# One bank and one reduce for the last query tile's row maxima, their minimum taken on the transposed row, and the rows' transfers issued by SyncE from head 22 on

## The chip, the cores and the metric

The kernel runs on one core of a Trainium2 chip. A core has TensorE (PE: matmuls and, beside them, weight loads, PEld), VectorE (DVE), ScalarE (ACT), GpSimd (POOL) and SyncE (SP). Each has a queue of its own, which it works through in order; DMA transfers are issued from the queues of ACT, POOL and SP and carried out by 16 DMA engines. The metric is the time on the device in microseconds (us), the median of several executions.

## The reference: what is computed

Attention in 8 batches of 8 heads, 576 positions, head size 64, with a mask by blocks of 64 (a query block sees its own and earlier key blocks), then a feed-forward part over the 4608 tokens, 512 wide inside 2048:

```python
scores = scale * np.matmul(q, k.transpose(0, 1, 3, 2))
mask = block_i >= block_j                 # blocks of 64 positions
scores = np.where(mask, scores, -1000000000.0)
scores = scores - np.max(scores, axis=-1, keepdims=True)
attn = np.exp(scores); attn = attn / (np.sum(attn, axis=-1, keepdims=True) + 1e-09)
x = (attn @ v) as 4608 x 512
h = x @ w_in                              # 512 x 2048
sp = np.maximum(h, 0.0) + np.log1p(np.exp(-np.abs(h)))
out = (h * erf(sp)) @ w_out               # 2048 x 512
```

What matters here is the maximum of each query's visible scores, which is subtracted before the exponential.

## The kernel before

The 64 heads (8 x 8) are passed in a loop over n; queries are cut into five tiles of 128 (the last has 64). `load_qk` brings a head's queries and keys (L383 and L385 from POOL's queue, L384 the copy `st` from SP's queue) into one of four buffers `qks[n % 4]`, and POOL works out their low parts (L388, L389). One partition of such a buffer, D + 4, is reserved for the negated maxima of the queries: a head's scores are computed twice, first in `maxes` to find the maxima, and then in `probs` with the maxima as one more row of the contraction (K = D + 5), so that PE itself subtracts them.

`maxes(n)` has the scores of the five query tiles in PSUM banks (L400), tile 0 and 1 in one bank, tiles 2 and 3 in one each, and the last tile's 64 queries in two banks: its 576 keys don't fit a bank of 512, so they are two halves of 288. DVE reduces each to a negated maximum per query (L403) in a column of `mx`: columns 0 to 3 for the first tiles, 5 and 6 for the halves of the last, of which L428 takes the minimum into column 4. Then PE transposes the five columns (L430), ACT rounds them into `mt`, five rows of 128 (L432), and ACT issues one transfer that lays these rows one behind the other into the head's buffer (L433, called the row). `probs(n)` can't begin before that has landed: its first product of each key tile, L446, reads the row; a second product L447 adds the low parts, and ACT takes the exponential (L451). L495 multiplies them with the values.

In iteration n of the head loop the steps of several heads are merged by fractional positions: the load of head n + 3, the maxima of head n + 2, the row of head n + 1, the probabilities of head n, and the products of earlier heads with the values. Beside them run, from head 9 on, the MLP's tiles of 256 tokens (up L190, the polynomial for erf(softplus) on ACT L159 to L162, DVE L163 to L165, ACT L166 and POOL L167, down L199, the sum with parts stored in `part_d` L240 to L249), and until head 23 the splitting of the weights into 16-bit parts (L112 to L147, by integer operations of DVE and activations of ACT). A scheduler turns priorities into the final order of each engine's queue, so an edit can move instructions that it doesn't touch. Ahead of the loop stand the maxima of heads 0 and 1, and head 0's row. The loads of raw weights and values wait for a one-element copy from tile 3's column of `mx` (L112 and L325), which keeps them behind the heads' loads. In iterations 0 and 1 there are dummy matmuls, ten each (L647), called "warm" in the trace.

Of the kernel before, what the change touches and what calls it, by code (L numbers as in the profile page):

```python
# [9 lines left out]
F32 = mybir.dt.float32  # L10
# [4 lines left out]
ALU = mybir.AluOpType  # L15
AX = mybir.AxisListType
# [7 lines left out]
def f32(ap):  # L24
    return ap.bitcast(F32)
# [7 lines left out]
def tile_attention_moe(ctx: ExitStack, tc: tile.TileContext, qk, v, w, maskrows, sels, out):  # L33
    nc = tc.nc
    B, H, D4, S = qk.shape
    D = D4 // 4
    NT, DM = out.shape
    NF = w.shape[0]
    P = 128
    NCC = DM // P  # L40
    SCALE = 0.125
    NQ = H // 4
# [221 lines left out]
    NB = 4  # L264
    qks = [wpool.tile([P, 4 * S + 64], F32R, name=f"qk{i}", bufs=1) for i in range(NB)]
# [28 lines left out]
    with tc.tile_pool(name="apool", bufs=2) as apool, tc.tile_pool(name="spool", bufs=1) as spool, \  # L294
            tc.tile_pool(name="ps_a", bufs=4, space=PSUM) as ps_a:
        pstage = [spool.tile([P, n], F32, name=f"p32_{i}") for i, n in enumerate(PN)]
        rss = [spool.tile([P, SH], F32, name=f"rs{i}") for i in range(3)]
        mxs = [spool.tile([P, 7], F32, name=f"mx{i}") for i in range(2)]

        def memsets():  # L300
            nc.gpsimd.memset(pstage[0][64:128, 768:], 0.0)
# [7 lines left out]
        def bank(name):  # L309

            turn.append(0)
            k = len(turn) % 8 if not loaded else 0
            if k in (2, 5):
                return ps_h.tile([P, 512], F32, tag="h", name=name)
            if k in (3,):
                return ps_o.tile([P, 512], F32, tag="o", name=name)
            return ps_a.tile([P, 512], F32, tag="a", name=name)
# [75 lines left out]
        def maxes(n):  # L393

            mx, K = mxs[n % 2], D + 4
            kh, qh = part(n, 2), part(n, 3)

            def mm(dst, i, k0, w_):
                r = min(P, S - i * P)
                nc.tensor.matmul(dst[:r, :w_], lhsT=qh[:K, i * P : i * P + r], rhs=kh[:K, k0 : k0 + w_], start=True, stop=True)  # L400

            def red(col, src, r=P):
                nc.vector.tensor_reduce(out=mx[:r, col : col + 1], in_=src, axis=AX.X, op=ALU.max, negate=True)  # L403

            def a():
                s = bank(f"s01_{n}")
                mm(s, 0, 0, 256)
                mm(s[:, 256:], 1, 0, 256)
                red(0, s[:, :128])
                red(1, s[:, 256:])  # L410

            def b():
                s = bank(f"s2_{n}")
                mm(s, 2, 0, 384)
                red(2, s[:, :384])

            def c():
                s = bank(f"s3_{n}")
                mm(s, 3, 0, 512)
                red(3, s)  # L420

            def d(j):
                s = bank(f"s4_{n}_{j}")
                mm(s, 4, 288 * j, 288)
                red(5 + j, s[:64, :288], 64)

            def e():
                nc.vector.tensor_reduce(out=mx[:64, 4:5], in_=mx[:64, 5:7], axis=AX.X, op=ALU.min)  # L428
                pt = bank(f"mt{n}")
                nc.tensor.transpose(out=pt[:5, :P], in_=mx[:, :5], identity=ident)  # L430
                mt = apool.tile([5, P], F32R, tag="mt", name=f"mt_{n}")
                nc.scalar.copy(mt, pt[:5, :P])  # L432
                nc.scalar.dma_start(f32(qks[n % NB][D + 4 : D + 5, 3 * S :]).rearrange("o (i p) -> o i p", p=P), f32(mt))  # L433

            return [a, b, c, lambda: d(0), lambda: d(1), e]

        def probs(n, out):

# [165 lines left out]
        def next_raw(src=None):  # L604
            if len(raws) < len(HALVES):
                fs = HALVES[len(raws)]
                raws[fs] = load_raw(*fs, apool, src)

        for n in range(2):
            *steps, rows[n] = maxes(n)  # L610
            for f in steps:
                f()
            if n == 0:
                v32 = load_v(0, 0, mxs[0][:1, 3:4])
                rows.pop(0)()
            next_raw(mxs[n][:1, 3:4])
        def late(kind, steps):

            def run(f):
# [30 lines left out]
        for n in range(N + 3):  # L650
            lists = []
            if n + NB - 1 < N:
                load, low = load_qk(n + NB - 1)
                lists += [(late("load", [load]), 0, LQ), (late("low", [low]), LQ, 1)]
            if n + 2 < N:
                *steps, rows[n + 2] = maxes(n + 2)
                lists.append((late("max", steps), 0, 1))
            if n + 1 in rows:
                lists.append((late("max", [rows.pop(n + 1)]), 0, 0.6))
            if n < N:  # L660
                prs[n] = []
                lists.append((late("prob", probs(n, prs[n])), 0, 1))
            qd = n // 4 + 1
            if n < 2:
                lists.append(([lambda v0=v32: scale_v(0, 0, *v0), lambda v0=v32: vs.__setitem__(0, prep_v(0, 0, *v0))][n : n + 1], 0.6, 0.8))
            if n % 4 == 1 and qd < N // 4:
                v32 = load_v(*divmod(qd, NQ), mxs[(n + 1) % 2][:1, 3:4])
            if n % 4 == 2 and qd < N // 4:
                lists.append((late("v", [lambda qd=qd: scale_v(*divmod(qd, NQ), *v32)]), 0, 1))
            if n % 4 == 3 and qd < N // 4:  # L670
                lists.append((late("v", [lambda qd=qd: vs.__setitem__(qd, prep_v(*divmod(qd, NQ), *v32))]), 0, 1))
            if n % 2 == 0 and 2 <= n <= N:
                j = n // 2 - 1
                qd, pp = divmod(j, 2)
                usbs[j] = apool.tile([P, S], F32, tag="usb", name=f"usb{j}", bufs=2)
                steps = pv(qd, pp, [prs.pop(2 * j), prs.pop(2 * j + 1)], vs[qd], usbs[j], rss[j % 3])
                lists.append((late("pv", steps), 0, 1))
                if pp == 1:
                    normals[n + 1] = qd
            if n in normals:  # L680
                qd = normals.pop(n)
                b, q_ = divmod(qd, NQ)
                lists.append((late("norm", normalise(b, q_, [usbs.pop(2 * qd), usbs.pop(2 * qd + 1)], [rss[2 * qd % 3], rss[(2 * qd + 1) % 3]])), 0.2, 0.8))
                if q_ == NQ - 1:
                    lists.append((late("norm", [lambda b=b: scale_b(b)]), 0, 0.2))
                    ready_at[n + 1] = (b + 1) * S // T
            ready = ready_at.get(n, ready)
            for _ in range(TOF.get(n, 0)):
                lists.append((late("conv", [conv]), 0, 1))
            if n in SCALE_AT:  # L690
                lists.append(([lambda n=n: scale_group(SCALE_AT[n])], 0, 0.1))
            if n in SPLIT:
                lists.append((late("conv", [split_next] * SPLIT[n]), 0.1, 1))
            if n < 2:
                lists.append(([warm] * WARM, 0, 1))
            lists.append((late("moe", [lambda: moe1(ready)] * RATE[0 if n < 10 else 1 if n < 20 else 2]), 0, 1))
            merge(*lists)
# [42 lines left out]
```

## Time and profile before

| | us |
|---|---|
| median of 3 executions | 1251.46 (1250.63 to 1252.27) |
| the profiled execution | 1253.77 |
| its span | 1252.0 |
| TensorE busy | 1169.7 (93%) |
| weight loads (PEld) | 811.0 (65%) |
| ScalarE busy | 865.4 (69%) |
| VectorE busy | 791.9 (63%) |
| GpSimd busy | 515.9 (41%) |

The span is the time between the first and the last instruction in the profile, and the execution's own time lies 1.77 us above it. Rows of groups read: line, engine, operation, out<-in with partitions x elements, count, then busy time, mean ns of one, and idle time ahead of them with what ended it. Rows of a timeline read: start, duration, engine, line, and in square brackets the idle time before with its releaser. ACTq and SPq are the queues' DMA issues. PE's busy time counts a matmul from its start to its modelled end, and neighbours overlap.

### The profile page before, as it was taken

What the parts mean: (1) busy time and instruction counts of PE and PEld (TensorE: products, weight loads), DVE (VectorE), ACT (ScalarE), POOL (GpSimd) and SP (SyncE); (2) the same over time, 40 slices, a digit from 0 to 9 for tenths busy, and PEclk for the clock granted to TensorE, in tenths of its full rate; (3) what the DMA queues carried; (4) which work ended last, traced back from release to release, by engine and by line L of the source; (5) the groups of instructions that cost most, each with busy time, mean ns of one, the idle gap of its engine ahead of it and who ended that gap; (6) DMA issues with size and microseconds to landing.
All of it is one profiled execution on the core that took longest, in us unless ns stands there. A gap on an engine that the chain in (4) does not pass through costs nothing.

```text
span 1252.0 us, 23446 instructions
## 1 busy us (share of the span) xinstructions
PE 1169.7 (93%) x9018; PEld 811.0 (65%) x9018; DVE 791.9 (63%) x1457; ACT 865.4 (69%) x1699; POOL 515.9 (41%) x486
## 2 busy tenths in 40 slices
PE   5788699989999999999999899999999999999896
PEld 2465466666666767767767677766777766666563
DVE  4677689787577666676657667666666644343433
ACT  1465577687676777877777677777777876666664
POOL 6455446545343444445444353545443313121211
PEclk9876799999999999999999999999999999999999
DMA  9988569744544455364454455455554121121211
GB/s 218 250 208 190 124 181 234 195 101 117 112 128 110 115 125 128 100 147 120 99 124 116 118 119 130 112 124 128 112 137 108 45 78 53 60 76 35 64 55 51
DMA packets 95741, 151.73 MB, mean 121 GB/s; under 512 B 7738, under 2 KB 44922, under 8 KB 95630
## 3 DMA queue, kind: packets, MB, share of 16 engines
q1 hardware_dynamic: 69840, 93.34, 25.7%
q0 software_dynamic: 25120, 56.66, 22.6%
q8 instruction: 71, 1.16, 0.4%
q10 hardware_dynamic: 670, 0.23, 0.2%
q14 instruction: 40, 0.33, 0.1%
HBM read 121.66 MB, written 28.31 MB: 120 GB/s over the span
## 4 chain that ended last, share of the span: by engine, by line
PE 49%; DVE 20%; ACT 18%; DMA 7%; issue 4%; POOL 1%; DVEq 0%; SPq 0%; POOLq 0%; ACTq 0%
PE m_h L190 16%; PE o L199 15%; PE u L495 5%; DVE m_r L163 4%; DVE m_r L164 4%; DVE m_r L165 3%; ACT m_r L160 3%; ACT m_r L162 3%; ACT m_r L161 3%; ACT m_r L159 3%; PE t L446 3%; PE s L400 3%; PE t L447 2%; DMA qk<-qk 2%; DMA qk<-mt 2%
## 5 line engine op out<-in xcount | busy, mean ns | idle before, releaser
L190 PE MATMUL m_h<-xh,w 128*128 128x256 f16 x2304 | 476.1, 276 | 19.5 <-DVE m_r L165 12.2
L190 PEld LDWEIGHTS <-w 128*128 128x128 f16 x3456 | 328.3, 99 | 158.1 <-issue 31.2
L199 PE MATMUL o<-w,m_gh 128*128 128x512 f16 x1152 | 334.1, 382 | 12.2 <-DVE pt L240 4.9
L167 POOL TENSOR_TENSOR m_gl<-m_r,m_gh 128x512 f16<-128x512 f32 x144 | 171.8, 1193 | 391.1 <-ACT m_gh L166 340.6
L190 PE MATMUL m_h<-xl,w 128*128 128x256 f16 x1152 | 316.8, 275 | 0.5 <-DMA xl<-x_d 0.5
L403 DVE TENSOR_REDUCE mx<-s 64x1 f32<-64x288 f32 (+4 forms) x384 | 174.5, 469 | 131.3 <-PE s L400 130.5
L163 DVE SCALAR_TENSOR_TENSOR m_r<-m_r,m_r 128x512 f32<-128x512 f32 x144 | 112.8, 783 | 197.3 <-ACT m_r L162 190.8
L199 PE MATMUL o<-w,m_gl 128*128 128x512 f16 x576 | 203.7, 384 | 0.3 <-POOL m_gl L167 0.3
L451 ACT ACTIVATE p<-t 128x288 f32<-128x288 f32 (+4 forms) x384 | 144.6, 384 | 79.4 <-PE t L447 69.1
L166 ACT CAST m_gh<-m_r 128x512 f16<-128x512 f32 x144 | 88.9, 617 | 157.2 <-DVE m_r L165 154.4
L446 PE MATMUL t<-qk 69*128 69x288 f32 (+4 forms) x384 | 168.2, 439 | 13.0 <-DMA qk<-mt 6.8
L400 PE MATMUL s<-qk 68*64 68x288 f32 (+3 forms) x384 | 150.1, 423 | 22.8 <-DMA qk<-qk 19.8
L159 ACT ACTIVATE m_r<-m_h,c,bs 128x512 f32<-128x512 f32 (+3 forms) x192 | 124.1, 666 | 44.5 <-PE m_h L190 41.4
L388 POOL TENSOR_TENSOR qk<-st,qk 64x576 fp32r<-64x576 f32 x64 | 95.9, 1499 | 127.2 <-DMA qk<-qk 124.5
L199 PEld LDWEIGHTS <-m_gh 128*128 128x128 f16 x1152 | 100.2, 98 | 67.6 <-issue 12.3
L164 DVE SCALAR_TENSOR_TENSOR m_r<-m_r 128x512 f32<-128x512 f32 x144 | 122.6, 852 | 3.3
L447 PE MATMUL t<-qk 128*128 128x288 f32 (+4 forms) x384 | 120.0, 313 | 0.0
L463 DVE TENSOR_TENSOR p<-p,p 128x832 f16<-128x832 f32 x80 | 81.7, 1022 | 58.0 <-ACT p L462 57.9
L389 POOL TENSOR_TENSOR qk<-st,qk 64x576 fp32r<-64x576 f32 x64 | 98.4, 1538 | 39.2 <-DMA qk<-qk 29.1
L161 ACT ACTIVATE m_r<-m_r,c 128x512 f32<-128x512 f32 x144 | 103.8, 721 | 2.7 <-ACT m_r L160 0.7
L162 ACT ACTIVATE m_r<-m_r,c 128x512 f32<-128x512 f32 x144 | 103.7, 720 | 2.3 <-ACT m_r L161 0.3
L160 ACT ACTIVATE m_r<-m_r,c 128x512 f32<-128x512 f32 x144 | 103.7, 720 | 1.6
(99 smaller groups left out, 1454.8 us busy)
## 6 DMA issues: line engine op xcount, KB each, us to landing
qk<-qk POOLq DMA_DIRECT2D x64, 432.0 KB, 5.0
st<-qk SPq DMA_DIRECT2D x64, 288.0 KB
qk<-qk POOLq DMA_DIRECT2D x64, 288.0 KB, 5.6
raw<-w SPq DMA_DIRECT2D x32, 512.0 KB
v<-v SPq DMA_DIRECT2D x16, 640.0 KB
x_d<-xs POOLq DMA_DIRECT2D x32, 288.0 KB, 3.3
xh<-x_d SPq DMA_DIRECT2D x36, 256.0 KB
xl<-x_d SPq DMA_DIRECT2D x36, 256.0 KB
```

Of the source, the lines that this page charges most:

```text
L159: nc.scalar.activation(r0s[:, :, lo:hi], h[:, :, lo:hi], AF.Tanh, bias=const(p1), scale=bss[b][g][:, 0:1])
L161: nc.scalar.activation(r0, r1, AF.Square, bias=const(b2), scale=a2)
L163: nc.vector.scalar_tensor_tensor(out=r0, in0=r0, scalar=c4, in1=r1, op0=ALU.add, op1=ALU.mult)
L164: nc.vector.scalar_tensor_tensor(out=r0, in0=r0, scalar=c5, in1=r0, op0=ALU.add, op1=ALU.mult)
L167: nc.gpsimd.tensor_tensor(out=gl, in0=r0, in1=gh, op=ALU.subtract)
L190: nc.tensor.matmul(h[:, k, :], lhsT=wf[:, a, sl], rhs=x[:, cc, :], start=cc == 0 and i == 0, stop=cc == NCC - 1 and i == 2)
L199: nc.tensor.matmul(o[c], lhsT=a[:, sl], rhs=wf[:, b_, :], start=u == u0 and k == 0 and not lo and b_ == 2, stop=u == u1 - 1 and k == nu - ...
L400: nc.tensor.matmul(dst[:r, :w_], lhsT=qh[:K, i * P : i * P + r], rhs=kh[:K, k0 : k0 + w_], start=True, stop=True)
L403: nc.vector.tensor_reduce(out=mx[:r, col : col + 1], in_=src, axis=AX.X, op=ALU.max, negate=True)
L446: nc.tensor.matmul(s[:kk, :w_], lhsT=kh[:K, ks], rhs=qh[:K, q0 : q0 + w_], start=True, stop=False)
L447: nc.tensor.matmul(s[:kk, :w_], lhsT=klh[:, ks], rhs=qhl[:, q0 : q0 + w_], start=False, stop=True)
L451: nc.scalar.activation(p32s[part][:kk, c : c + w_ - skip], s[:kk, skip:w_], AF.Exp, scale=SCALE)
```

## The change

`mx` shrinks from seven columns to five: tile i is reduced into column (i + 1) % 5, so the last tile is in column 0. The last tile uses one bank: a product of 128 queries (the last 128) with keys 288 to 575 fills rows 0 to 127, then the product of the last 64 queries with keys 0 to 287 overwrites rows 0 to 63. So rows 64 to 127 hold the last queries' scores with the later keys, rows 0 to 63 those with the earlier ones, and one reduce of 128 partitions takes both. After the transpose, row 0 of `mt` holds the two partial maxima side by side, and DVE takes their minimum there (a piece of 64 elements on one partition). The row goes out as two transfers: four rows of 128, which don't need that minimum, and the 64 elements of row 0. Both are issued by ACT for heads below 22 and by SP from 22 on. The copies that hold the loads back read column 4, again tile 3's.

```diff
-        mxs = [spool.tile([P, 7], F32, name=f"mx{i}") for i in range(2)]
+        mxs = [spool.tile([P, 5], F32, name=f"mx{i}") for i in range(2)]
...
-            def red(col, src, r=P):
-                nc.vector.tensor_reduce(out=mx[:r, col : col + 1], in_=src, axis=AX.X, op=ALU.max, negate=True)
+            def red(i, src):
+                col = (i + 1) % 5
+                nc.vector.tensor_reduce(out=mx[:, col : col + 1], in_=src, axis=AX.X, op=ALU.max, negate=True)
...
-            def d(j):
-                s = bank(f"s4_{n}_{j}")
-                mm(s, 4, 288 * j, 288)
-                red(5 + j, s[:64, :288], 64)
+            def d():
+                s = bank(f"s4_{n}")
+                nc.tensor.matmul(s[:, :288], lhsT=qh[:K, S - P :], rhs=kh[:K, 288:], start=True, stop=True)
+                mm(s, 4, 0, 288)
+                red(4, s[:, :288])
 
             def e():
-                nc.vector.tensor_reduce(out=mx[:64, 4:5], in_=mx[:64, 5:7], axis=AX.X, op=ALU.min)
                 pt = bank(f"mt{n}")
                 nc.tensor.transpose(out=pt[:5, :P], in_=mx[:, :5], identity=ident)
                 mt = apool.tile([5, P], F32R, tag="mt", name=f"mt_{n}")
                 nc.scalar.copy(mt, pt[:5, :P])
-                nc.scalar.dma_start(f32(qks[n % NB][D + 4 : D + 5, 3 * S :]).rearrange("o (i p) -> o i p", p=P), f32(mt))
-
-            return [a, b, c, lambda: d(0), lambda: d(1), e]
+                nc.vector.tensor_tensor(out=mt[:1, :64], in0=f32(mt[:1, :64]), in1=f32(mt[:1, 64:]), op=ALU.min)
+                row = f32(qks[n % NB][D + 4 : D + 5, 3 * S : 3 * S + S])
+                dma = (nc.scalar if n < 22 else nc.sync).dma_start
+                dma(row[:, : 4 * P].rearrange("o (i p) -> o i p", p=P), f32(mt[1:]))
+                dma(row[:, 4 * P :], f32(mt[:1, :64]))
+
+            return [a, b, c, d, e]
...
-            next_raw(mxs[n][:1, 3:4])
+            next_raw(mxs[n][:1, 4:5])
```

The scheduler moves instructions in response. The first place is PE's queue at the very start. In the names, s01_1 are the scores of head 1's tiles 0 and 1, s4 those of the last tile, mt0 the transposed maxima of head 0, qk1 head 1's buffer. Before, from row 5 of the queue on:

```order
L400 MATMUL s4_0_1_216<-qk0_128 64x288
L400 MATMUL s4_1_1_245<-qk1_129 64x288
L400 MATMUL s4_1_0_242<-qk1_129 64x288
L647 LDWEIGHTS ones32_78
L647 MATMUL warm_251<-ones32_78 32x512
L647 LDWEIGHTS ones32_78
L647 MATMUL warm_251<-ones32_78 32x512
L400 MATMUL s01_2_263<-qk2_130 128x256
L430 MATMUL mt0_223<-ident_77,mx0_146 5x128
L400 MATMUL s01_1_231<-qk1_129 128x256 x2
L400 MATMUL s2_1_236<-qk1_129 128x384
```

After, the same stretch, where the line of "..." stands for nineteen more pairs of a weight load and a warm matmul:

```order
L425 MATMUL s4_0_213<-qk0_128 128x288
L400 MATMUL s4_0_213<-qk0_128 64x288
L400 MATMUL s01_1_230<-qk1_129 128x256 x2
L400 MATMUL s2_1_235<-qk1_129 128x384
L652 LDWEIGHTS ones32_78
L652 MATMUL warm_248<-ones32_78 32x512
...
L400 MATMUL s01_2_260<-qk2_130 128x256 x2
L400 MATMUL s3_1_238<-qk1_129 128x512
L431 MATMUL mt0_220<-ident_77,mx0_146 5x128
L425 MATMUL s4_1_241<-qk1_129 128x288
L400 MATMUL s4_1_241<-qk1_129 64x288
L451 MATMUL t0_0_0_256<-qk0_128 128x288
```

The transpose of head 0 stood behind two of the twenty warm matmuls and now stands behind all of them, and head 0's first product with the row (L451 of the changed kernel) follows three instructions later.

The second place is DVE's queue at the start. Before, head 0's minimum (L428) is taken ahead of all of head 1's reduces:

```order
L403 TENSOR_REDUCE mx0_146<-s4_0_1_216 64x1
L325 COPY v0_0_219<-mx0_146 1x1
L112 COPY raw0_0_228<-mx0_146 1x1
L428 TENSOR_REDUCE mx0_146<-mx0_146 64x1
L403 TENSOR_REDUCE mx1_147<-s4_1_0_242 64x1
L403 TENSOR_REDUCE mx1_147<-s4_1_1_245 64x1
```

After, head 0's minimum (L434) comes behind all five of head 1's reduces:

```order
L404 TENSOR_REDUCE mx0_146<-s4_0_213 128x1
L325 COPY v0_0_217<-mx0_146 1x1
L112 COPY raw0_0_227<-mx0_146 1x1
L404 TENSOR_REDUCE mx1_147<-s01_1_230 128x1 x2
L404 TENSOR_REDUCE mx1_147<-s2_1_235 128x1
L404 TENSOR_REDUCE mx1_147<-s3_1_238 128x1
L404 TENSOR_REDUCE mx1_147<-s4_1_241 128x1
L434 TENSOR_TENSOR mt_0_222<-mt_0_222 1x64
L112 COPY raw0_1_245<-mx1_147 1x1
```

The minimum moved from before the transpose to behind it, and on DVE it stands behind head 1's reduces of s3 and s4.

The third place is SP's queue where the rows' transfers come to it. The first two of them in the changed kernel, with what stands around them (v32 are values, xh and xl the attention's output read back, ob a part sum that is stored):

```order
L326 DMA v32_3_0_3042<-v 128x1280
L437 DMA qk2_130<-mt_22_3086 1x4x128
L438 DMA qk2_130<-mt_22_3086 1x16x4
L384 DMA st_26_3492<-qk 128x576
L243 DMA part_d_58<-ob0_2_0_3172 128x512
L243 DMA part_d_58<-ob0_2_1_3234 128x512
L222 DMA xl1_1_3351<-x_d_57 128x4x256
L222 DMA xh1_1_3349<-x_d_57 128x4x256
L384 DMA st_27_3657<-qk 128x576
L437 DMA qk3_131<-mt_23_3335 1x4x128
L438 DMA qk3_131<-mt_23_3335 1x16x4
```

Without those four rows the stretch is the same in the kernel before, where ACT issues them: the transfers of head 23 stand behind the load `st` of head 27.

More of the change, by code (lines that the diff above doesn't have):

```diff
@@ L613, in tile_attention_moe @@
             if n == 0:
-                v32 = load_v(0, 0, mxs[0][:1, 3:4])
+                v32 = load_v(0, 0, mxs[0][:1, 4:5])
                 rows.pop(0)()
-            next_raw(mxs[n][:1, 3:4])
+            next_raw(mxs[n][:1, 4:5])
         def late(kind, steps):
@@ L666, in tile_attention_moe @@
             if n % 4 == 1 and qd < N // 4:
-                v32 = load_v(*divmod(qd, NQ), mxs[(n + 1) % 2][:1, 3:4])
+                v32 = load_v(*divmod(qd, NQ), mxs[(n + 1) % 2][:1, 4:5])
             if n % 4 == 2 and qd < N // 4:
```

## The prediction

> **What bounds the kernel now.** I read the page first, then a table of busy time by stage, then the chain of waits, then the timelines at the places where the change acts. The page:
>
> ```profile
> span 1252.0 us, 23446 instructions
> PE 1169.7 (93%) x9018; PEld 811.0 (65%) x9018; DVE 791.9 (63%) x1457; ACT 865.4 (69%) x1699; POOL 515.9 (41%) x486
> PE 49%; DVE 20%; ACT 18%; DMA 7%; issue 4%; POOL 1%; DVEq 0%; SPq 0%; POOLq 0%; ACTq 0%
> ```
>
> TensorE (PE) is busy 93% of the span, and the chain that ended last runs through it for half. The busy time of each engine by stage, with the granted clock and the DMA share behind it, shows that this isn't so from the start:
>
> ```profile
> 0.00:40.00 40.00, 19.79 (x78) 11.23 (x78) 18.39 (x45) 8.82 (x24) 22.20 (x43) 0.96 1.08 230
> 40.00:120.00 80.00, 70.41 (x444) 47.09 (x442) 58.78 (x137) 47.43 (x128) 38.94 (x37) 0.76 0.90 219
> 120.00:160.00 40.00, 29.54 (x187) 19.65 (x187) 26.67 (x56) 23.50 (x48) 20.03 (x17) 0.76 0.61 132
> 160.00:320.00 160.00, 151.44 (x1159) 103.03 (x1157) 128.75 (x243) 118.19 (x263) 79.58 (x69) 0.99 0.61 156
> 320.00:1010.00 690.00, 675.68 (x5575) 482.03 (x5573) 462.00 (x838) 511.67 (x991) 304.62 (x280) 1.00 0.48 117
> ```
>
> The columns are PE, PE's weight loads, DVE, ACT, POOL, clock, DMA share, GB/s. Up to 120 us the DMA engines are full, and PE has 30 us without work. From 160 us on PE leaves only 8.6 + 14.3 = 22.9 us free in 850. The row maxima that the change touches appear in the chain of waits as transfers qk<-mt (the row into the query buffer), at these places among its 55 longest pieces:
>
> ```profile
> 16.84 8.15 DMA raw<-w
> 26.44 3.44 DMA qk<-mt
> 31.44 7.53 DMA qk<-mt
> 52.06 4.92 DMA qk<-mt
> 86.54 4.23 DMA qk<-mt
> 94.05 5.46 DMA qk<-mt
> ```
>
> So a row's transfer sets the pace five times, all before 100 us. Later no transfer of a row is late; there I look at what PE waits for. Between 160 and 1010 us (line, releaser, us, times, longest):
>
> ```profile
> PE m_h L190 <- DVE m_r L165: 10.4, 15, 2.1
> PE rt L556 <- DVE mx L403: 2.3, 3, 1.1
> PE t L446 <- DVE mx L403: 2.0, 3, 0.9
> PE rb L575 <- DVE m_r L165: 1.6, 2, 1.0
> PE mt L430 <- DVE mx L428: 0.8, 1, 0.8
> ```
>
> That is 17.1 of the 22.9 us, all behind DVE. It is everything that a lighter DVE can give there.
>
> **The change part by part.** All lines named are those of before; the sum is made against the profiled execution, 1253.77 us (span 1252.0 and 1.77 around it), which lies 2.31 above the median of 1251.46.
>
> *Lighter DVE, fewer issues on ACT.* The groups by shape:
>
> ```profile
> L403 DVE TENSOR_REDUCE mx<-s 64x1 f32<-64x288 f32 x128 | 56.3, 443 | 23.2 <-PE s L400 23.0
> L428 DVE TENSOR_REDUCE mx<-mx 64x1 f32<-64x2 f32 x64 | 9.0, 141 | 1.0
> L400 PEld LDWEIGHTS s<-qk 68*128 68x128 f32 x256 | 48.4, 202 | 31.4 <-issue 11.2 <-DMA qk<-qk 4.3 <-ACT a L126 2.9
> L400 PEld LDWEIGHTS s<-qk 68*64 68x64 f32 x128 | 18.1, 142 | 11.1 <-issue 4.0 <-DVE mx L403 0.6 <-ACT mt L432 0.4
> ```
>
> Per head two reduces of 443 ns become one over 128 partitions and the same 288 columns; the duration goes by columns, so I take 443 again. L428 (141 ns) goes; the new minimum of two 64-element pieces in one row isn't in the trace, and I take 150 ns, near L428, between 0 and 443. Net 443 + 141 - 150 = 434 ns per head, 64 heads: 28 us of DVE's 792. From head 22 on ACT also loses its issue, 0.70 us x 42 = 29 us of 865 (row of 18.46 below). ACT and DVE aren't PE: what counts is the 17.1 us above. The row transform's own part is small in it (0.8 + 2.0 + 2.3); the largest, 10.4, are 15 single waits at the MLP's element chain, which a DVE 5% lighter shortens somewhat. I take **-3** (a sixth), bounds 0 and -9. On PE one of two weight loads per head has 128 columns, 202 instead of 142 ns; 64 x 0.06 = 3.8 us if bare, but weight loads overlap the matmul before them, so 0. The two products keep their 288 columns each, and so their time.
>
> *The start.* PE in order of time, before:
>
> ```profile
> 9.32 1.99 PE L400 MATMUL s<-qk 68*128 68x256 f32 x6 [9.32 <-DMA qk<-qk]
> 14.64 0.71 PE L400 MATMUL s<-qk 68*64 68x288 f32 x2 [3.33 <-DMA qk<-qk]
> 17.72 0.41 PE L430 MATMUL mt<-ident,mx 128*5 128x128 f32 x1
> 19.46 1.46 PE L647 MATMUL warm<-ones 128*32 128x512 f16 x3
> 21.57 3.25 PE L647 MATMUL warm<-ones 128*32 128x512 f16 x10
> 24.75 0.40 PE L446 MATMUL t<-qk 69*128 69x288 f32 x1
> 30.01 0.37 PE L446 MATMUL t<-qk 69*128 69x288 f32 x1 [0.89 <-DMA qk<-mt]
> ```
>
> Head 0's transpose (mt) came after two of the twenty dummy matmuls ("warm"); now it stands behind all twenty, as PE's order shows. From 14.64: three products of head 1 (0.33 each by the first row) to 15.6; twenty warm ones at 0.325 (the row of ten) 6.5 us, to 22.1 (9.7 by the row of three, which is colder); three more products at 0.2, and the transpose at 0.3: it ends near 23.0, where it ended at 18.13: +4.9. Behind it come the cast, head 1's last two reduces, for which the minimum waits on DVE, and two issues instead of one:
>
> ```profile
> 18.46 0.71 ACTq L433 DMA_DIRECT2D qk<-mt  x1
> 21.68 0.69 DVE L403 TENSOR_REDUCE mx<-s 128x1 f32<-128x512 f32 x1 [0.76 <-PE s L400]
> ```
>
> Two issues of 0.7 after a cast ending at 23.3 end at 24.8. Then the landing: the row issued from 26.44 to 27.14 let PE go at 30.01, 2.9 later; so the first L446 comes at 27.7 and not at 24.75. There the ten warm matmuls covered the landing, and this cover is gone. **+3**, bounds 0 (the row landed the moment its issues end, 24.8) and +6.9 (the slowest landing of the chain, 7.53 from an issue at 24.1); I take 2.9 because that row is the nearest in time.
>
> The Trainium skill ("TensorE: Matmul & The Clock Gate", Part 1, the HAM clock gate) says the array runs at half rate until it has been busy for about 3.4 us, then at full rate. By that, 20 matmuls of 512 columns would be about 6.0 us (an estimate from its 427 and 216 ns each) and the term +2.5; the trace agrees in kind, since three take 0.49 each and ten later ones 0.325.
>
> *Second issue and minimum in the heads before 22.* The row now has two transfers on ACT, the second behind DVE's minimum. At each of the five pieces of the chain above that is 0.70 + 0.15, less L428's 0.14, about +0.7 and some queueing on DVE: 5 x 0.7 = 3.5. The DMA engines are full there (1.08 and 0.90), so a lag may only shorten the next wait for a load. **+2**, a little over half of it, bounds 0 and +6 (with 0.5 us of queueing each).
>
> *ACT held at the second issue.* The queue is in order: while the second transfer's issue waits for DVE's minimum, all exps, MLP activations and copies behind it on ACT wait, and so do PE's users of them. While the second weight group is split, heads 11 to 21, that split's integer work stands ahead of the minimum. Head 13's row was issued at 166.08 on ACT; ahead of its minimum DVE now has, by its order, both pieces of the weight split that were here:
>
> ```profile
> 168.57 1.66 DVE L122 SCALAR_TENSOR_TENSOR w<-a,w 128x512 int32<-128x512 int32 x1
> 171.18 0.74 DVE L121 TENSOR_SCALAR w<-raw 128x512 int32<-128x512 int32 x2
> ```
>
> By those times ACT would stand at the second issue from 166.8 to 171.9, 5 us, with the exp of head 12 behind it. DVE and ACT will drift together, and ACT had 42 us free between 160 and 320. **+1.5**, bounds 0 and +5.
>
> *Transfers by SP from head 22 on.* SP's queue is in order too: the row now stands behind the loads and stores that the schedule puts ahead of it. Head 23 is the tightest, behind the load st of head 27:
>
> ```profile
> 307.86 0.70 ACTq L433 DMA_DIRECT2D qk<-mt  x1
> 310.44 0.35 SPq L384 DMA_DIRECT2D st<-qk  x1
> 325.66 0.33 SPq L243 DMA_DIRECT2D part_d<-ob  x1
> 320.17 0.49 PE L446 MATMUL t<-qk 69*128 69x288 f32 x1
> ```
>
> It was issued at 307.86 and can now go at 310.8, 3 us later; the slowest landing of the chain, 7.53, ends at 318.3, before PE's first use at 320.17. Hidden: **0**. SP's loads behind the rows wait for DVE's minimum, but SP had issued nothing from 310.8 to 325.66, so 0 as well.
>
> Sum: +3 + 2 + 1.5 - 3 = +3.5: 1257.3 in the profiled execution's frame, **1255.0** in the median's.
>
> **The rivals.** 0.2% is 2.5 us, about what a measurement of this kernel can tell from no change: 1249.0 to 1254.0 is "same".
>
> *A, the start is absorbed (same).* Up to 120 us the loads fill the DMA engines, so heads later than their rows wait for loads anyway: the start's +3 falls to +1, the second issue's +2 to +1, with ACT's +1.5 and the relief's -3: +0.5, 1252. For it speaks the DMA share of 0.90 to 1.08. Against it, the chain crosses five rows there, and head 4's load needs head 0's buffer free.
>
> *B, the relief is larger (faster).* DVE loses 0.43 us and ACT 0.70 per head from head 22 on; if the order of the queues turns these into earlier products, about half of DVE's 0.43 x 42 = 18 us shows, -9, and with +4 left of the early terms the sum is -5: 1246.5. Against it, PE is busy 675.68 of 690 us there: only 14.3 us are to be had at all, if busy is taken at its word. For it, PE's weight loads fill only 482 of these 690, so busy PE may hide waits. The Trainium skill ("Trainium Kernel Development and Optimization", its note on reading a trace) says as much: matmul busy time is a bad metric, as matmuls are pipelined, and the share of LDWEIGHTS is a good one; by that 30% and not 2% would be open. The trace can't decide between them before the change is seen.
>
> *C, ACT is held (much slower).* If each of the heads 11 to 21 holds ACT by 1 us that PE feels, +10 in place of +1.5: +12, 1263.5. It decides where the waits of ACT for the minimum exceed ACT's free 42 us between 160 and 320, some 4 us a head; head 13's 5 us speaks for it, but the other heads' predecessors on DVE end earlier.
>
> **How the numbers follow.** Forecast (the four terms as taken, slower) 0.35; A 0.26; B 0.30; C 0.09. Slower is 0.35 + 0.09 = 0.44, same 0.26, faster 0.30. The forecast's own range is 1254 to 1260. The range asked for reaches to B's lower end, relief at its bound of -9 and +2.6 early, 1245, and to C's 1264.
>
> **What would show it.** Start: the transpose of head 0 ends near 23.0 and head 0's first L446 product starts near 27.7. If it starts by 25.5, the first term is wrong. Second issue: chain pieces qk<-mt before 100 us longer by about 0.7 each. Hold: ACT's waits for DVE's minimum in heads 11 to 21 sum to over 10 us, but PE's waits for ACT grow by under 3. Relief: PE free from 320 to 1010 falls from 14.3 to about 12, and rows for DVE m_r from 10.4 to 8 or so. SP: no wait of PE for qk<-mt after 320 us. The prediction is wrong if the stage 320 to 1010 gets shorter by over 5 us (B), or if up to 320 us nothing is lost (A or B).

## The result

The changed kernel takes 1262.1 us (median of 15 executions, 1254.45 to 1271.29), the kernel before 1251.46 (15 executions beside them, 1245.71 to 1256.19). The ratio is 1.0099, 95% interval 1.0077 to 1.0120: by the ratio 12.4 us slower (9.6 to 15.0), while the two medians are 10.6 us apart. All ratios leave out executions over 1.5% above the fastest of their kernel, so a ratio need not be that of the two medians beside it. The forecast was +3.5, in a range of 1245 to 1264. The sign was right and that range held; the forecast's own range, 1254 to 1260, did not, and the loss is about three times what the sum gave.

The profiled execution of the changed kernel took 1261.63 us. Its page:

```profile
span 1259.8 us, 23617 instructions
PE 1173.5 (93%) x9018; PEld 820.3 (65%) x9018; DVE 787.6 (63%) x1393; ACT 864.8 (69%) x1699; POOL 514.7 (41%) x486
PE 47%; DVE 19%; ACT 18%; DMA 9%; issue 5%; POOL 1%; SPq 0%; DVEq 0%; POOLq 0%; ACTq 0%
```

DVE is 4 us lighter and not 28. Two of its groups say why:

```profile
L404 DVE TENSOR_REDUCE mx<-s 128x1 f32<-128x288 f32 x64 | 28.8, 451 | 27.7 <-PE s L400 27.5
L434 DVE TENSOR_TENSOR mt<-mt 1x64 fp32r<-1x64 f32 x64 | 38.4, 600 | 17.1 <-ACT mt L433 17.1
```

The wide reduce took 451 ns, as worked out (443); the minimum took 600 on average and not 150, four times the estimate and above its upper bound of 443, and DVE stood another 17.1 us ahead of it, until ACT's cast was done. In the chain DMA went from 7 to 9%. The stages, in the columns of before:

```profile
0.00:40.00 40.00, 22.04 (x72) 14.23 (x72) 14.97 (x36) 7.82 (x20) 20.09 (x40) 0.85 0.98 206
40.00:120.00 80.00, 63.70 (x424) 44.79 (x425) 59.41 (x113) 43.01 (x122) 39.21 (x36) 0.73 0.95 223
120.00:160.00 40.00, 32.90 (x191) 23.22 (x192) 33.44 (x72) 27.25 (x56) 18.28 (x17) 0.71 0.72 147
160.00:320.00 160.00, 145.88 (x1054) 99.31 (x1054) 116.60 (x214) 111.06 (x247) 73.39 (x65) 0.93 0.61 150
320.00:1010.00 690.00, 678.31 (x5617) 484.82 (x5614) 463.59 (x813) 514.93 (x999) 311.13 (x282) 1.00 0.48 118
```

Up to 320 us PE does less in every stretch but the first and that of 120 to 160, at a lower clock (0.93 against 0.99 in 160 to 320). Behind it, it does a little more: free time from 320 to 1010 us fell from 14.3 to 11.7, where the prediction had about 12. PE at the start, in order of time:

```profile
14.60 1.09 PE L400 MATMUL s<-qk 68*128 68x256 f32 x3 [3.52 <-DMA qk<-qk]
15.62 7.17 PE L652 MATMUL warm<-ones 128*32 128x512 f16 x20
23.42 0.27 PE L431 MATMUL mt<-ident,mx 128*5 128x128 f32 x1
28.50 0.61 PE L451 MATMUL t<-qk 69*128 69x288 f32 x1 [4.54 <-DMA qk<-mt]
```

The transpose ends at 23.69 (forecast 23.0), head 0's first product with the row starts at 28.50 (27.7), and the wait that had been covered stands in the open, 4.54 us. The two issues of that row on ACT, and the minimum on DVE:

```profile
24.01 0.64 ACTq L437 DMA_DIRECT2D qk<-mt  x1
25.69 0.57 ACTq L438 DMA_DIRECT2D qk<-mt  x1
```

```profile
24.59 1.07 DVE L434 TENSOR_TENSOR mt<-mt 1x64 fp32r<-1x64 f32 x1
```

```profile
24.20 1.39 POOL L388 TENSOR_TENSOR qk<-st,qk 64x576 fp32r<-64x576 f32 x1 [0.66 <-DMA qk<-qk]
```

The second issue waits 1.04 us for the minimum, which waits for head 1's reduces, as worked out. That the minimum itself lasts 1.07 us was not: the last line is POOL's subtraction for a head's low part, which was running when the minimum began, and the minimum ends at 25.66, 0.08 us after it. It is so in all of the trace. Of the 64 minima, 34 began while a tensor_tensor of POOL (L388, L389 or L167) was running, and each of them ended 74 to 81 ns after it, whatever was left of it: 222 to 1421 ns, 946 on average. The other 30 took 203 to 214 ns. So some 25 of the 38.4 us are DVE held by POOL inside the instruction, and a minimum that isn't held takes 0.2 us. At the start this delays the row by some 0.9 us (1.07 less the 0.2 of an unheld minimum).

The rest has no term in the sum: I compared when each head's first product with the row starts (the first of its six L451, L446 before). Head 0 is 3.8 us late against before, head 9 also 3.8, head 19 7.6, head 21 16.3, head 63 7.9. So in this pair of profiles the larger part is lost between heads 19 and 21, where I had no term.

What stands there: the first tiles of the MLP's next group need xh and xl, loaded by SP from where the attention wrote them. SP's queue around head 19, before and then after:

```profile
237.01 5.98 SPq L243 DMA_DIRECT2D part_d<-ob  x2
243.17 0.37 SPq L222 DMA_DIRECT2D xh<-x_d  x1
243.59 0.56 SPq L222 DMA_DIRECT2D xl<-x_d  x1
245.36 21.63 SPq L384 DMA_DIRECT2D st<-qk  x3
```

```profile
251.36 0.33 SPq L384 DMA_DIRECT2D st<-qk  x1
251.87 0.38 SPq L222 DMA_DIRECT2D xh<-x_d  x1
252.29 0.51 SPq L222 DMA_DIRECT2D xl<-x_d  x1
254.75 0.43 SPq L243 DMA_DIRECT2D part_d<-ob  x1
```

The load st of head 23 and the second of two stores part_d have changed places around the four loads of xh and xl: st now stands ahead of them, the store behind. Measured from head 19's first product (244.7 before, 252.3 after), xl is issued 1.1 us later than it was. PE of the changed kernel then stands twice:

```profile
260.46 0.37 PE L190 MATMUL m_h<-xl,w 128*128 128x256 f16 x1 [4.02 <-DMA xl<-x_d]
277.89 0.37 PE L190 MATMUL m_h<-xh,w 128*128 128x256 f16 x1 [3.26 <-DVE m_r L165]
```

xl takes 8.2 us from its issue to its use; before, PE used it 4.3 us after the issue and didn't wait. The second wait, for the element chain's m_r, I read as that chain running dry behind the first; this isn't shown by itself. The stretch from head 19 to head 22, before and after:

```profile
244.70:300.10 55.40, 50.55 (x378) 35.96 (x377) 44.03 (x88) 43.92 (x88) 25.33 (x22) 1.00 0.49 117
```

```profile
252.30:315.00 62.70, 54.81 (x381) 37.92 (x379) 42.10 (x84) 44.56 (x89) 24.09 (x21) 0.92 0.46 104
```

The same heads, 7.3 us longer, at a clock of 0.92 in place of 1.00: the trace has the clock at 0.50 from 260.0 to 263.4 and from 277.1 to 283.9, around the ends of the two waits, and at 1.00 between and behind.

### The profile page after: what moved, and what is told of

The parts are those of the page before. It is cut to its first block, busy times and chain, and to the rows that moved or that the text cites. A ratio compares the mean times of both kernels' runs of the same rounds, so it can differ in the third digit from the quotient of the medians.

```text
span 1259.8 us, 23617 instructions
## 1 busy us (share of the span) xinstructions
PE 1173.5 (93%) x9018; PEld 820.3 (65%) x9018; DVE 787.6 (63%) x1393; ACT 864.8 (69%) x1699; POOL 514.7 (41%) x486
## 3 DMA queue, kind: packets, MB, share of 16 engines
q1 hardware_dynamic: 71520, 93.44, 25.6%
## 4 chain that ended last, share of the span: by engine, by line
PE 47%; DVE 19%; ACT 18%; DMA 9%; issue 5%; POOL 1%; SPq 0%; DVEq 0%; POOLq 0%; ACTq 0%
PE m_h L190 16%; PE o L199 15%; PE u L500 5%; DVE m_r L164 4%; DVE m_r L163 4%; DVE m_r L165 3%; ACT m_r L160 3%; ACT m_r L159 3%; ACT m_r L162 3%; PE t L451 3%; ACT m_r L161 3%; PE t L452 2%; DMA qk<-qk 2%; PE s L400 2%; DMA qk<-mt 2%
## 5 line engine op out<-in xcount | busy, mean ns | idle before, releaser
L190 PE MATMUL m_h<-xh,w 128*128 128x256 f16 x2304 | 476.8, 276 | 11.8 <-DVE m_r L165 11.7
L199 PE MATMUL o<-w,m_gh 128*128 128x512 f16 x1152 | 334.6, 382 | 13.4 <-DVE pt L240 6.1
L167 POOL TENSOR_TENSOR m_gl<-m_r,m_gh 128x512 f16<-128x512 f32 x144 | 174.0, 1209 | 413.9 <-ACT m_gh L166 357.4
L404 DVE TENSOR_REDUCE mx<-s 128x1 f32<-128x128 f32 (+4 forms) x320 | 146.6, 475 | 102.5 <-PE s L400 101.7
L451 PE MATMUL t<-qk 69*128 69x288 f32 (+4 forms) x384 | 171.1, 447 | 17.5 <-DMA qk<-mt 14.1
L388 POOL TENSOR_TENSOR qk<-st,qk 64x576 fp32r<-64x576 f32 x64 | 95.0, 1485 | 147.2 <-DMA qk<-qk 143.2
L400 PE MATMUL s<-qk 68*128 68x256 f32 (+3 forms) x320 | 117.2, 404 | 21.6 <-DMA qk<-qk 15.3
L452 PE MATMUL t<-qk 128*128 128x288 f32 (+4 forms) x384 | 123.1, 322 | 0.0
L164 DVE SCALAR_TENSOR_TENSOR m_r<-m_r 128x512 f32<-128x512 f32 x144 | 114.1, 793 | 3.2
L389 POOL TENSOR_TENSOR qk<-st,qk 64x576 fp32r<-64x576 f32 x64 | 98.4, 1538 | 31.2 <-DMA qk<-qk 28.3
```

What stands on the lines that cost most here:

```text
L164: nc.vector.scalar_tensor_tensor(out=r0, in0=r0, scalar=c5, in1=r0, op0=ALU.add, op1=ALU.mult)
L167: nc.gpsimd.tensor_tensor(out=gl, in0=r0, in1=gh, op=ALU.subtract)
L190: nc.tensor.matmul(h[:, k, :], lhsT=wf[:, a, sl], rhs=x[:, cc, :], start=cc == 0 and i == 0, stop=cc == NCC - 1 and i == 2)
L199: nc.tensor.matmul(o[c], lhsT=a[:, sl], rhs=wf[:, b_, :], start=u == u0 and k == 0 and not lo and b_ == 2, stop=u == u1 - 1 and k == nu - ...
L404: nc.vector.tensor_reduce(out=mx[:, col : col + 1], in_=src, axis=AX.X, op=ALU.max, negate=True)
L451: nc.tensor.matmul(s[:kk, :w_], lhsT=kh[:K, ks], rhs=qh[:K, q0 : q0 + w_], start=True, stop=False)
```

## The experiments

Most runs use one switch: the old code of the last tile, the minimum and the row is kept beside the new, and `NEW(n)` chooses for each head. In the traces all five queues of the run from head 22 on have the order of before up to 263 us, and those of the run below head 22 the order of after up to 280 us, so the switch itself moves nothing. Each kernel was timed against before on the same chip; the intervals of the ratios are about 0.3% wide each way (4 us), and differences of a few us between two runs are within them.

```diff
+        def NEW(n):
+            return n >= 22
...
-            return [a, b, c, lambda: d(0), lambda: d(1), e]
...
+            return [a, b, c, d, e] if new else [a, b, c, lambda: d_old(0), lambda: d_old(1), e_old]
```

**From head 22 on.** `NEW(n)`: `n >= 22`.

> The change made only for heads 22 to 63 (one bank, one reduce, minimum behind the transpose, rows issued by SyncE); heads 0 to 21 as before, and the queues' order up to there is that of before. Theory (the loss of the whole change lies in heads 0 to 21, and the lighter steady stage gives back what the lag of the profiled run shows between head 21 and the end, +16.3 to +7.8): 7 to 9 us faster than before. Rival 1 (what was regained after head 21 was only the slack of a late run, which a run that isn't late does not have): within 2 us of before. Rival 2 (rows on SyncE cost in the steady stage): slower than before.

Measured: 1244.14 us against 1247.24, ratio 0.9974 (0.9942 to 1.0006). A gain of about 3 us if any (the interval runs from 7 faster to 1 slower), and not clearly the 7 to 9 of the theory: it seems that more than half of what the lag gave back was slack. Rival 1 was nearer.

**Below head 22.** `NEW(n)`: `n < 22`.

> The change made only for heads 0 to 21, with both transfers of the row issued by ScalarE; heads 22 to 63 as before. Theory: the loss alone, 14 to 18 us slower than before (the lag at head 21 was +16.3), so slower than the whole change by 4 to 8. Rival 1 (the late heads absorb a lag by themselves): about as slow as the whole change, 8 to 12 us over before.

Measured: 1267.58, ratio 1.0155 (1.0116 to 1.0194), some 19 us from six executions. The loss lies in the early heads, and rival 1's 8 to 12 is below the interval. Its profiled execution, 1260.63, is the shortest of the six.

**From head 2 on.** `NEW(n)`: `n >= 2`.

> The whole change but for heads 0 and 1, which are done as before, so that head 0's transpose stands again behind two of the dummy matmuls and head 0's first product near 24.8 us. Theory (the start's lag of 3.8 us is carried to the end, since the chain runs through the rows): 3 to 5 us faster than the whole change, about 6 slower than before. Rival (the loads that fill the DMA engines up to 120 us absorb it): as slow as the whole change, within 1.5 us.

Measured: 1249.99, ratio 1.0030 (0.9997 to 1.0062). Without the change in heads 0 and 1 two thirds of the loss are gone, more than the theory's 3 to 5 us and against the rival's 1.5.

**Rows by SyncE alone.** The kernel before, with

```diff
-                nc.scalar.dma_start(f32(qks[n % NB][D + 4 : D + 5, 3 * S :]).rearrange("o (i p) -> o i p", p=P), f32(mt))
+                (nc.scalar if n < 22 else nc.sync).dma_start(f32(qks[n % NB][D + 4 : D + 5, 3 * S :]).rearrange("o (i p) -> o i p", p=P), f32(mt))
```

> The kernel before with one edit: the row's single transfer is issued by SyncE from head 22 on. Theory (hidden behind PE's work, and ACT is not the bound there): within 2 us of before. Rival (ACT's 0.70 us per head was what the steady stage waited for): 4 to 8 us faster, as much as the heads from 22 on give in the other run. Rival 2 (rows late behind loads on SyncE): slower, with PE waiting for the row after 320 us.

Measured: 1248.46, ratio 1.0014 (0.9982 to 1.0047). As forecast: neither gain nor loss that the interval shows.

**A later head 0, with PE kept warm.** The kernel before, with

```diff
...
+                for _ in range(40):
+                    warm()
                 rows.pop(0)()
...
             if n < 2:
-                lists.append(([warm] * WARM, 0, 1))
+                pass
```

> The kernel before with its dummy matmuls moved and doubled: forty of them (20 more than before) in one block ahead of head 0's transpose, so that it ends some 5 us later; one transfer per row, L428 and all else as before, and PE kept warm. Theory (what the start of the change costs is the lateness of head 0, which gates the buffer of head 4's load, and the load of raw weights behind head 1's maxima): 4 to 9 us slower than before, with the DMA share from 20 to 40 us near 0.8 in place of 1.0. Rival (the cost is PE's clock, which falls to 0.70 there when PE waits idle for the row): within 2.5 us of before, since PE isn't idle.

Measured: 1250.6, ratio 1.0015 (0.9985 to 1.0045). The transpose of head 0 ended at 21.3 and its first product started at 28.00, 3.3 us later than before; the DMA share from 20 to 40 us was 0.97, where the whole change has 0.79. PE wasn't kept warm: the granted clock from 20 to 40 us was 0.66 (0.93 before, 0.70 in the whole change). So neither this lateness nor a cold PE there costs anything clear by itself; the lower DMA share of the whole change wasn't reproduced.

**The dummy matmuls later.** The whole change, with

```diff
-            if n < 2:
+            if n in (1, 2):
                 lists.append(([warm] * WARM, 0, 1))
```

> The whole change, with the twenty dummy matmuls issued in iterations 1 and 2 in place of 0 and 1, so that head 0's transpose has none ahead of it; the row's two transfers and the minimum stay. Theory (lateness of head 0): head 0's first product near 24 us, and 6 to 9 us faster than the whole change. Rival (clock): PE idles between the transpose and the row and is cold for heads 0 to 2, so no more than 2 us faster than the whole change.

Measured: 1258.16, ratio 1.0075 (1.0045 to 1.0105). Head 0's first product started at 25.27, yet most of the loss stays. The warm block isn't its main cause; the interval leaves open whether it has a part.

**From head 9 on.** `NEW(n)`: `n >= 9`.

> The change made from head 9 on; heads 0 to 8 as before; rows by ScalarE below head 22. The runs so far give 7 us for heads 2 to 21. Theory (ScalarE held at the second issue while VectorE splits weights, heads 9 to 21): this costs as much as the change from head 2 on, 2 to 5 us over before. Rival (the second issue in the heads up to 8, where the rows are on the chain): this is as fast as the change from head 22 on, 2 to 4 us under before.

Measured: 1254.01, ratio 1.0034 (1.0004 to 1.0064): as from head 2 on. The second issue of heads 2 to 8 costs nothing that shows beside these intervals; what heads 9 to 21 cost, 0.6% over the run from head 22 on, is the larger part.

**From head 9 on, rows by SyncE.** The same, with

```diff
-                dma = (nc.sync if n >= 22 else nc.scalar).dma_start
+                dma = (nc.sync if n >= 9 else nc.scalar).dma_start
```

> As the run from head 9 on, with both transfers of every changed row issued by SyncE, so that ScalarE never waits for VectorE's minimum. Theory (ScalarE held): 4 to 7 us faster than the run from head 9 on, 2 to 4 us under before. Rival (no hold that counts, or SyncE's queue makes the rows late among the weight loads): as that run or slower.

Measured: 1253.88, ratio 1.0042 (1.0015 to 1.0069): no gain. ScalarE's hold isn't the cost that the theory took it for; a part of 1 or 2 us can't be excluded. That left where the loss lies, and not why; the starts of the heads in all profiles showed the same step between heads 19 and 22, in every run with the change at head 20. In each of these six PE waits there for xl, 1.8 to 4.0 us, and at one place 3.2 to 3.3 us for m_r, as long behind a short first wait as behind a long one; in the four profiles without it, PE has no wait for xl there.

**From head 20 on, and from head 21 on.** `NEW(n)`: `n >= 20` and `n >= 21`. They differ by one head, and the queues by 22 rows on PE and, on SP, by st of head 23 and the store part_d, which change places around the four loads; this swap is all that SP's two queues differ by.

> The change from head 20 on (heads 20 and 21 with ScalarE's transfers, from 22 on with SyncE's). With head 20 in the change, the order of SyncE's queue puts the load st of head 23 ahead of the four loads of the MLP's tiles 2 and 3 (xh, xl), as in the whole change; this queue and 22 rows of PE's are what tells it from the run from head 21 on. Theory (the loss between heads 19 and 22, 61 us in all runs with that order and 55 in all without, comes with this order): PE waits 2 to 4 us for xl and 3 us for m_r near 255 and 275 us, heads 19 to 22 take 60 to 62 us, and the run is 5 to 6 us slower than the run from head 21 on, 1 to 4 over before. Rival (the loss belongs to the minimum and the second issue of each of the heads 9 to 21): within 1.5 us of the run from head 21 on, under before.

> The change from head 21 on; SyncE's queue has the loads of the MLP's tiles 2 and 3 ahead of st of head 23, as before. Theory: no wait of PE for xl, heads 19 to 22 in 53 to 56 us, 2 to 5 us faster than before, the fastest of these. Rival (a loss per head): as the run from head 20 on.

Measured from head 20 on: 1249.28, ratio 0.9997 (0.9961 to 1.0032); its profiled execution took 1256.93, so I read from it only what the other profiles show too. From head 21 on: 1242.87, ratio 0.9969 (0.9941 to 0.9997). The stretch from head 19 to head 22 in the two:

```profile
243.80:304.90 61.10, 54.15 (x378) 37.69 (x377) 41.83 (x84) 43.82 (x88) 24.71 (x21) 0.92 0.45 106
```

```profile
248.30:302.50 54.20, 49.96 (x379) 35.63 (x377) 44.01 (x84) 44.13 (x89) 24.77 (x21) 1.00 0.51 114
```

And PE's waits there in the first; the second has no wait for xl, and its longest for m_r is 1.57:

```profile
251.02 0.37 PE L190 MATMUL m_h<-xl,w 128*128 128x256 f16 x1 [3.08 <-DMA xl<-x_d]
269.13 0.37 PE L190 MATMUL m_h<-xh,w 128*128 128x256 f16 x1 [3.18 <-DVE m_r L165]
```

One head's step switches 6.9 us of this stretch. The ratios are 0.28% apart, some 3.5 us, and their intervals overlap: the profiles settle this, and the times agree with it without showing it. The run from head 21 on is 0.31% (0.03 to 0.59) faster than before, some 4 us.

**st of head 23 by ScalarE.** As from head 20 on, with

```diff
-                nc.sync.dma_start(st, qk[b, h, : 2 * D])
+                (nc.scalar if n == 23 else nc.sync).dma_start(st, qk[b, h, : 2 * D])
```

> As the run from head 20 on, with the load st of head 23 alone issued by ScalarE, so that SyncE's queue has no st ahead of the four loads; PE's order changes in 6 rows. Theory (the place of st in SyncE's queue, which waits for a free buffer and holds the loads back): the wait for xl is under 1 us, heads 19 to 22 take 54 to 57 us, and the time is that of the run from head 21 on. Rival (PE reaches the tile's products too early in any case, or the transfers share the DMA engines whatever their queue): PE waits 2 us or more for xl, and the time is that of the run from head 20 on.

Measured: 1250.94, ratio 1.0015 (0.9989 to 1.0042), 0.46% above the run from head 21 on, and the stretch from head 19 to head 22 took 58.2 us, between the two. ACT issued st at 237.45, xl followed on SP, and PE waited again:

```profile
237.45 0.39 ACTq L391 DMA_DIRECT2D st<-qk  x1
```

```profile
246.15 0.37 PE L190 MATMUL m_h<-xl,w 128*128 128x256 f16 x1 [3.23 <-DMA xl<-x_d]
```

Head 19's first product started at 238.8 and xl was issued at 238.64, 0.2 us ahead of it; from head 20 on it was 0.1, from head 21 on 1.2. So st's place in SP's queue isn't what holds xl; the theory fell here. Nor is the place of the store, which stands ahead of the loads again in this run, as before. What the loads stood behind was that store: xh follows it by 0.5 us before, from head 21 on and here (242.67, 246.17 and 237.72), and here it went out 1 us later against head 19; why it did wasn't taken apart. The rival has two halves. PE doesn't come too early: without the wait it would be at the product 4.1 us after head 19's start here, from head 20 on and in the whole change, against 3.1 before and 3.6 from head 21 on. But xl takes 7.3 to 8.2 us from issue to use in these three, against 4.3 and 4.8 there, without a wait. In all three st was issued ahead of it, and POOL's transfers of head 23 followed 0.5 to 0.6 us behind its issue; before and from head 21 on, st came behind it and POOL's 1.6 us behind. That xl shares the DMA engines with these loads is the rival's other half. It fits, but it is argued and not shown: no run moves POOL's transfers alone.

**Heads 0 and 1 alone.** `NEW(n)`: `n < 2`.

> The change in heads 0 and 1 alone; all others as before. PE's start is that of the whole change: head 0's transpose behind the twenty dummy matmuls. Theory (the start's loss stands by itself; the whole change less the change from head 2 on gives 8 us): 5 to 10 us slower than before. Rival (the start alone costs the 3.8 us by which head 0's first product is late, or less, and the rest came with the heads behind it): 0 to 4 us slower than before.

Measured: 1246.6, ratio 1.0002 (0.9971 to 1.0033). Head 0's first product started at 26.23, 1.5 us late. By itself the start costs nothing that shows: the interval runs from 3.6 us faster to 4.1 slower.

All profiles together, by the starts of the heads' first products with the row (us):

| run | head 0 at | 0 to 9 | 9 to 19 | 19 to 22 | 22 to 63 |
|---|---|---|---|---|---|
| before | 24.7 | 85.3 | 134.6 | 55.4 | 717.8 |
| from 22 on | 25.0 | 87.8 | 128.0 | 52.9 | 709.2 |
| SyncE alone | 24.7 | 91.3 | 133.6 | 55.5 | 715.7 |
| later head 0 | 28.0 | 83.1 | 136.0 | 55.7 | 715.7 |
| heads 0, 1 | 26.2 | 88.3 | 127.4 | 54.7 | 712.4 |
| from 21 on | 25.0 | 89.5 | 133.8 | 54.2 | 711.4 |
| from 20 on | 24.8 | 89.1 | 130.0 | 61.1 | 714.8 |
| st by ScalarE | 24.4 | 84.4 | 130.0 | 58.2 | 711.9 |
| from 9 on | 24.9 | 89.2 | 132.5 | 61.2 | 713.9 |
| from 9 on, SyncE | 25.0 | 86.9 | 137.7 | 60.0 | 710.3 |
| from 2 on | 23.1 | 80.4 | 134.8 | 61.2 | 711.1 |
| warm later | 25.3 | 87.3 | 134.0 | 60.2 | 709.9 |
| below 22 | 25.8 | 89.3 | 136.6 | 60.0 | 712.8 |
| after | 28.5 | 85.4 | 138.4 | 62.6 | 710.9 |

Single profiles scatter: before and the run from head 22 on, whose queues are the same up to there, differ by 2.5 and 6.6 us in the first two stretches. Means of the runs that have the change in a stretch against those that don't: 9 to 19, 135.7 of six (the last six rows) against 131.7 of eight, +4.0, with an error of about 1.5; 19 to 22, 60.9 of seven (from 20 on and the last six rows) against 54.7 of six, +6.2, and no run of the one kind within 4 us of one of the other (st by ScalarE, between them, left out); 22 to 63, 711.5 of nine against 714.9 of five, -3.4, with an error of about 1.2. Head 9 starts at 114.0 on average in the four runs with the change in heads 0 and 1 and at 112.7 in the eight with heads 0 to 8 and the warm block as before: +1.3, where these eight alone range from 108.8 to 116.0 (later head 0 and the run from head 2 on, with 111.1 and 103.5, are in neither group).

## Why the prediction was right in sign and short in size

*The start, +3.* The mechanism was right up to head 0's first product: transpose 23.69, two issues, an uncovered landing, head 0 3.8 us late. That 28.50 is so near 27.7 is in part two errors that cancel: the issues ended at 26.26 and not 24.8, 0.9 of it by the minimum's wait for POOL, and the row landed 2.2 us after them and not 2.9. That the lag would be carried to the end was not right: +1.3 at head 9 on average, and 0.2 us (-3.6 to +4.1) for heads 0 and 1 by themselves. This is what rival A said of the start. The dummy matmuls took 7.17 us for twenty; the row of ten had given 6.5, and the Trainium skill ("TensorE: Matmul & The Clock Gate", Part 1) an estimate of 6.0. The trace was the slowest of the three: behind a wait of 3.52 us, the first thirteen gaps from one to the next are 0.40 to 0.43 us, the last six 0.22.

*Second issue, +2.* The pieces qk<-mt of the chain:

```profile
25.69 3.90 DMA qk<-mt
37.15 7.61 DMA qk<-mt
75.15 4.84 DMA qk<-mt
89.62 6.26 DMA qk<-mt
98.87 4.30 DMA qk<-mt
```

26.9 us in five pieces against 25.6 before: not 0.7 each. From head 2 on and from head 9 on cost the same (1.0030 and 1.0034), so heads 2 to 8 give this term nothing that shows; with intervals of 4 us each way, +2 isn't excluded.

*ACT held at the second issue, +1.5.* The hold is there, and by its signs as forecast: over heads 0 to 21 the second issue starts 13.4 us later than the first ends, in sum, 10.4 of it in heads 11 to 21 (forecast: over 10), while PE's waits for ACT from 120 to 320 us grew by 1.5 (forecast: under 3). In one head it is as much as I feared for head 13, where it was 1.17. It is head 18:

```profile
230.67 0.60 ACTq L437 DMA_DIRECT2D qk<-mt  x1
236.18 0.54 ACTq L438 DMA_DIRECT2D qk<-mt  x1
```

But no run shows that it costs anything: the one that takes the issues off ACT is no faster, within some 4 us. I had also looked at one direction only. DVE's queue is in order too, and waits for ACT's cast, 17.1 us in all (the group above), with the reduces behind it held as well; and the minimum waits a further 25 us for POOL. Where the +4.0 of heads 9 to 19 come from, these waits or the order, no run tells apart.

*The step that failed* is the assumption that the change's only work between heads 9 and 22 was the minimum and the second issue, at the row itself. I read the new order at three places, and in SP's queue only where the row's own transfers stand. There were no rows of the change at the place where it costs most: loads of the MLP and a load of a later head passed each other, PE waits 4.0 and 3.3 us, and 6.2 us go. This term was missing, and it is larger than any that I had. That it comes with head 20's step is shown by the runs from head 20 and from head 21 on; which of the rows that this step moves makes xl late is not.

*Rows by SyncE, 0.* Right as far as the interval tells: 1.0014 (0.9982 to 1.0047) alone, and no wait of PE for a row after 320 us.

*Relief, -3.* Right: -3.4 by the stretch; the time, 0.9974 (0.9942 to 1.0006), agrees, but its interval just includes no gain. That it was right is partly luck: DVE was to lose 28 us and lost 4. The mis-sized piece is the minimum: 0.15 us forecast, 0.20 by itself, 0.60 with its waits for POOL. The 17.1 us from which the -3 was taken were also not everything behind DVE: three more rows of the same view of before (L123, L135 and L240) add 3.0. PE's wait for the element chain, its largest, fell from 8.5 to 5.6 us between 320 and 1010 us. Between 160 and 1010 it went from 10.4 to only 8.8, since 3.3 of it stand at head 20, and the second row is new:

```profile
PE m_h L190 <- DVE m_r L165: 8.8, 10, 3.3
PE m_h L190 <- DMA xl<-x_d: 4.0, 1, 4.0
```

Rival B wanted 9 of it. The rule that stood beside it (the Trainium skill, "Trainium Kernel Development and Optimization", on reading a trace: PE's busy time is a bad metric) would have left 30% open; no run here gained more than 8.6 us from head 22 to 63 (717.8 to 709.2), within the 14.3 that PE's busy time leaves. This fits busy time but doesn't decide, since no run was made to shorten PE's own work.

*Rival C* had the size, 1263.5, by a mechanism of which the runs show no cost.

*The sign was in good part luck.* Of the forecast's own terms the runs show +1.3 for the start, nothing clear for the second issue and the hold, and -3.4 for the relief. They come out positive only if more than half of the +4.0 of heads 9 to 19 belongs to the hold or the second issue, which isn't shown; what made the kernel clearly slower wasn't in the sum.

*What stays open.* The stretches give +1.3 + 4.0 + 6.2 - 3.4 = 8.1 us, the times 12.4 (9.6 to 15.0). The parts don't add either: heads 0 and 1 alone 0.2 us, from head 2 or 9 on about 4, all of it 12.4, and below head 22 even 19. As the runs stand, heads 0 and 1 cost some 8 us only if those behind them are changed as well. The mean granted clock goes along with it in two cases (0.958 in the timed runs of the whole change and of the change below head 22, 0.965 to 0.971 in all others), but the run with the warm block later has 0.968 and is still 0.75% over before. SP's queue of the whole change also has raw weights and loads st in another order at 41 to 54 and 93 to 124 us, and weights and a store at 201 to 215 us; no run switches these places one by one. The cause of this part stays open.

## What to carry to other kernels

A change that removes and adds instructions lets a scheduler reorder things that it doesn't touch; price the new order over the whole queue of each DMA-issuing engine, above all where loads pass each other near their first use. A step moved from ahead of a cross-engine hand-over to behind it makes two in-order queues wait for each other, here 13.4 us on ACT and 17.1 on DVE, though no run shows what that costs. A small instruction isn't priced by its size alone: ask what the other engines run while it does. And where a change gains in one stage and loses in another, switch it by stage: from head 21 on it is 0.3% faster than before (0.03 to 0.59), as a whole 1% slower.

## What the runs showed of the hardware

The minimum of two 64-element pieces on one partition took 203 to 214 ns in the 30 cases in which no tensor_tensor of POOL was running when it began, and in the other 34 it ended 74 to 81 ns after POOL's did, up to 1421 ns after its start. It is the same from head 2 on, with 30 of 62 minima held in this way, and from head 21 on, with 26 of 43; the rest took 202 to 214 ns.

A max reduce out of PSUM took 451 ns over 128 partitions and 443 over 64, both of 288 columns. The row cut in two cost ACT 0.60 + 0.54 us of issue in the median, against 0.70 for the one transfer.

A load that PE used 4.3 us after its issue, without a wait, took 7.3 to 8.2 us in three runs (the whole change, from head 20 on, st by ScalarE) in which it went out about 1 us later and nearer to other loads. In the stretch of the changed kernel with two waits of PE of 4.0 and 3.3 us the mean granted clock was 0.92, against 1.00 before.
